# A planned top-k attention with a rational feed-forward layer: 512-wide passes over the first weight matrix, and longer planned TensorE steps for row tiles 8 to 21

## The chip, the cores and the metric

One core of one Trainium2 chip runs the whole kernel as one program. The time is that of the device in microseconds (us), the median of several executions. A profiled execution gives a trace, and its span runs from the first to the last instruction.

## The reference

Attention over 8 batches, 8 heads, 576 positions and a head size of 64, where each row keeps its 32 largest scores, followed by a layer whose activation is a ratio of two polynomials:

```
scores = q @ k.T / 8
kth    = 32nd largest score of each row
attn   = softmax of the scores >= kth
x      = attn @ v                      # heads side by side: 4608 x 512
h      = x @ w_in                      # w_in 512 x 2048, float64
g      = (a0 + a1*h + a2*h^2 + a3*h^3) / (1 + |b0|*|h| + |b1|*h^2 + 1e-6)
out    = g @ w_out                     # w_out 2048 x 512, float64
```

q, k, v, a and b are float32. Both weight matrices arrive as 64-bit words, so the kernel turns them into 32-bit numbers on the chip.

## The kernel before, in words

**Tiles.** A row tile is 128 query rows of one head (a mixed tile: the last 64 rows of two heads). There are 288, numbered in the order of work. TensorE makes a tile's scores (`scores`, lines 577 to 589), ScalarE copies them out of PSUM, and VectorE finds the 32nd largest (lines 595 to 638) and the masked probabilities (line 694). TensorE transposes these (line 792) and multiplies them with v (`multiply`, line 825) for two row blocks of one head pair at a time. Tiles 0 to 15 are the first two row blocks of all eight heads, 16 to 19 are mixed, and 20 begins the next two row blocks.

**The layer.** When all heads of 256 rows are done they form a chunk. A chunk runs in 8 groups: a hidden product with w_in (line 967, three passes with high and low parts), the ratio on ScalarE, GpSimd and VectorE, and a product with w_out (lines 1127 and 1134).

**The weights.** `weight_block` takes one block of 128 x 512 float64 words: 16 blocks of w_in and 16 of w_out. A block of w_in comes in two loads of 128 x 256 words into the tiles that later hold the high and low parts (`win_h`, `win_l`). Then each half takes these steps: `low` (ScalarE, line 393, into a PSUM bank), `high` (VectorE, line 398), `sign` and `size` (ScalarE, lines 404 and 408), `join` (GpSimd, line 412). After both halves the block is split into a high part (line 274 or 276) and a low part (line 434). The PSUM bank is one of the two with the tag "mm", which the transposes, `multiply` and the hidden products also use. It goes back when both `size` steps are done.

**The order.** `Plan` simulates the engines while the program is written. Every step has an engine, a planned length, a key, steps that it waits for, and buffers that it takes and gives. `choose` gives a free engine the ready step with the lowest key. A step that is not critical stands back when a critical one with a lower key comes within LOOK. The order found this way is the fixed order of each engine's queue and of the DMA queue of SyncE (SP); the lengths have no other effect. The key of row tile n is n times T, with T 5.084. The entries of KEY move a kind of step against this: KL the load and split of k, QL that of q and of the mixed tiles' input, VL the load of v, PT the transposes, AV the product with v, EU and EW the ratio, PJ the product with w_out, WL the load of w_out's low parts, MS the later chunks.

**Buffers.** There are two buffers for v (tag "v"), given back by the last product with them (line 894), and one staging buffer for the loads of k and q (tag "kr"), given back when the low part is split off (lines 494 and 534).

Of the kernel before, what the change touches and what calls it, by code (L numbers as in the profile page):

```python
# [17 lines left out]
AX = mybir.AxisListType  # L18
PSUM = bass.MemoryType.PSUM

KEY = {'XM': 1, 'LN': 12, 'UV': 'DVE', 'UK': -552.455, 'B0': ('POOL',), 'B1': ('POOL', 'DVE'), 'B2': ('DVE', 'POOL'), 'B3': ('DVE', 'POOL'), 'WH': ('POOL', 'ACT'), 'XH': ('POOL', 'ACT'), 'TH': 0, 'EU': -5.754, 'HW': 256, 'Q0': ('POOL', 'ACT'), 'Q1': ('POOL',), 'SPLIT': (0, 2, 4, 6), 'XS': 1, 'RH': ('ACT',), 'p2': ('POOL',), 'p4': ('POOL',), 'ratio': ('POOL',), 'ratio_low': ('POOL',), 'URG': -48.538, 'PT': -11.07, 'AV': -5.694, 'MOE': 38.884, 'LOOK': 0.321, 'T': 5.084, 'KL': -2.162, 'PJ': 39.271, 'WL': -16.714, 'EX': 28.932, 'EW': 11.969, 'ALT': {'ACT': 0.086, 'DVE': 78.012, 'POOL': 2.27}, 'WG': 4.183, 'QL': -8.645, 'PACE': 10.97, 'MS': -1.055, 'NM': ('POOL',), 'WD': ('POOL', 'ACT'), 'LP': ('POOL',), 'VL': -3.335}
NEG = -3.0e38
NB = 8

# [154 lines left out]
def tile_topk_attention__then__rational_ffn(  # L179
# [48 lines left out]
    def add(*args, **kwargs):  # L228
        return plan.add(*args, **kwargs)
# [21 lines left out]
    pe_r = lambda n: max(0.109, n / 2230 + 0.003)  # L251
    pe_f = lambda n: 2 * max(0.109, n / 1200 + 0.003)
    pe_t = 0.109
    dma = lambda n, words: max(0.52 * n, words * 4 / 260e3)


# [59 lines left out]
    tiny = const.tile([P, 1], F32, name="tiny")  # L316
    nc.gpsimd.memset(tiny, 1e-9)

    win_h, win_l = {"nm": "win_h"}, {"nm": "win_l"}

    def own(win, c, e):
        def tile_of(dtype=F32R):
            nm = f"{win['nm']}{c}_{e}"
            x = const.tile([P, 512], dtype, tag=nm, name=nm)
            if dtype == F32R:
                win[c, e] = x
            return x
        return tile_of

# [21 lines left out]
    def weight_block(src, r0, e0, split, key, nm):  # L351
        rows = src[r0 : r0 + P, e0 : e0 + 512]
        o = Obj()
        f64 = rows.dtype != F32
        hi, lo, away = split
        plain = lo is None and away is None
        hold = [Hold("t") for _ in range(1 if lo is not None else 2)]
        xhold, turn = Hold("mm", 2), [Hold("wt")]

        def words(i, dtype=F32):  # L360
            return buf(hold[i], [P, 512], dtype, f"w_{nm}_{i}")

        if not f64:

            def load():
                o.w = hi if plain else words(0)
                o.low = words(1, F32R) if away is not None else lo if plain else lo()
                o.hi = hi if plain else hi()
                nc.sync.dma_start(o.w, rows)

            hold = [] if plain else hold
            last = [add("SP", dma(1, P * 512), load, key=key, take=hold)]
        else:

            def load():
                to = [words(i) for i in range(2)] if lo is None else [hi(F32), lo(F32)]
                o.parts = []
                for i, e in enumerate(range(0, 512, 256)):
                    r = to[i].bitcast(I32)
                    nc.sync.dma_start(r, rows[:, e : e + 256].bitcast(I32))  # L380
                    r = r.rearrange("p (e t) -> p e t", t=2)
                    o.parts.append((slice(e, e + 256), r[:, :, 0], r[:, :, 1]))

            ld = add("SP", dma(2, P * 1024), load, key=key, take=hold + turn if lo is None else [])
            last, first, final = [], [], []
            for i in range(2):

                def low(i=i):
                    es, low, high = o.parts[i]
                    if i == 0:  # L390
                        o.bits = bank(xhold, [P, 512], f"wb_{nm}")
                        o.w = words(0) if lo is not None else hi if plain else hi(F32)
                    nc.scalar.activation(o.bits[:, es], low.bitcast(U32), AF.Identity, scale=STEP, bias=two_)

                def high(i=i):
                    es, low, high = o.parts[i]
                    x = o.bits[:, es].bitcast(I32)
                    nc.vector.scalar_tensor_tensor(
                        x, high, 3, x, op0=ALU.logical_shift_left, op1=ALU.bitwise_xor
                    )  # L400

                def sign(i=i):
                    es, low, high = o.parts[i]
                    nc.scalar.activation(high.bitcast(F32), high.bitcast(F32), AF.Sign)

                def size(i=i):
                    es, low, high = o.parts[i]
                    nc.scalar.activation(o.w[:, es], o.bits[:, es], AF.Abs)

                def join(i=i):  # L410
                    es, low, high = o.parts[i]
                    nc.gpsimd.tensor_tensor(
                        out=o.w[:, es], in0=o.w[:, es], in1=high.bitcast(F32), op=ALU.mult
                    )

                s1 = add("ACT", act(256) + 0.15, low, [ld] + first, key + 1,
                         take=[] if first else [xhold] + (hold if lo is not None else []))
                first = [s1]
                s2 = add("DVE", dve(256), high, [s1], key + 1)
                s3 = add("ACT", act_sb(256), sign, [s2], key + 1)  # L420
                s4 = add("ACT", act(256), size, [s2], key + 2, give=[xhold])
                last.append(
                    add("POOL", pool_t(256), join, [s3, s4], key + 2, give=hold[i : i + 1] + turn[0 : i] if plain else [])
                )

        def high_part():
            if lo is not None and f64:
                o.hi, o.low = hi(), lo()
            elif f64:
                o.hi, o.low = words(0, F32R), words(1, F32R)  # L430
            affine(o.hi, o.w, 1.0, 0.0)

        def low_part():
            engine().tensor_tensor(out=o.low, in0=o.w, in1=o.hi.bitcast(F32), op=ALU.subtract)

        def high_again():
            affine(hi(), o.hi.bitcast(F32), 1.0, 0.0)

        if plain:
            return last  # L440

        s = add(one(512, 0, KEY['WH']), None, high_part, last, key + 3)
        if away is None:
            return [add(two(512, *KEY["LP"]), None, low_part, [s], key + 3, give=hold)]
        s = add(two(512, *KEY["LP"]), None, low_part, [s], key + 3)
        steps = [
            add("SP", dma(1, P * 512), lambda: nc.sync.dma_start(away, o.low.bitcast(F32)), [s],
                key + 3, give=hold[1:] + turn if f64 else hold)
        ]
        if f64:  # L450
            steps.append(add(one(512, 0, KEY['WH']), None, high_again, [s], key + 3, give=hold[0:1]))
        return steps
# [3 lines left out]
    def add_weights(key0, gap):  # L456
        n = 0
        blocks = []
        for e in range(0, DFF, 512):
            for c in range(HP):  # L460
                split = *(own(win, c, e // 512) for win in (win_h, win_l)), None
                blocks.append((("i", c, e // 512), w_in, c * P, e, split))
            for f in range(4 * (e // 512), 4 * (e // 512) + 4):
                split = (wout.get(f) or own_out(f), None, wout_l.get(f))
                blocks.append((("o", f), w_out, f * P, 0, split))
        for n, (name, *args) in enumerate(blocks):
            w_steps[name] = weight_block(*args, key0 + n * gap, f"w{n}")
# [97 lines left out]
    def add_tile(t):  # L565
# [131 lines left out]
            )  # L697

        if u.mixed:
            s = add("PE", 2 * pe_f(HF), scores, [kv.mload, prev.s], key - 3.2, take=[shold],  # L700
                    give=[kv.mhold], crit=True)
        else:
            s = add("PE", 0.07 + 4 * pe_r(HF), scores, [kv.load[t.h], u.pair.q.load, prev.s], key - 3.2, take=[shold],
                    give=[kv.khold, u.pair.q.hold], crit=True)
        prev.s = s
        e = add("ACT", act(S), evacuate, [s], key - 2.6, take=[sbhold], give=[shold], crit=True)
# [50 lines left out]
    def add_values(u):  # L757
# [108 lines left out]
        for i in ([0, 2] if u.mixed else [0, 1, 2]):  # L866
# [5 lines left out]
            bh = Hold("mm")  # L872
            n = NJ if i < 2 else 2
            kk = KEY['PT'] + (u.tiles[0].key + T if i == 0 else key + 0.4 * i)
            x = add("PE", n * pe_t, transpose(i), dep, kk, take=[bh] + ([] if at else [thold[i]]))
            tp.append(x)
            x.give = [u.phold]
            if i == 2:
# [10 lines left out]
        m = None  # L889
        cuts = [[0, 1, 2], [3, 4]] if u.mixed or lone else [[0, 1], [2, 3], [4]]  # L890
        for cs in cuts:
            m = add("PE", len(cs) * n_av, multiply(cs), [m] if m else pair.ev + [pair.vload], key + KEY['AV'],
                    take=[] if m else [avh] + ([] if u.chunk.parts or u.mixed else [u.chunk.hold]))
        m.give = [pair.vhold] + [thold[0]] + ([] if u.mixed else [thold[1]])
        m2, n = m, u.nq * len(pair.units)
# [457 lines left out]
```

## Time and profile before

| | |
|---|---|
| Median of 3 runs | 1546.0 us (1544.91 to 1546.16) |
| Profiled execution | 1545.54 us, span 1543.8 us |
| TensorE (PE) busy | 1431.8 us, 93% |
| VectorE (DVE) busy | 1383.6 us, 90% |
| ScalarE (ACT) busy | 1358.1 us, 88% |
| GpSimd (POOL) busy | 1150.2 us, 75% |
| Mean granted TensorE clock | 0.974 |

Engines run beside each other, so a share of busy time says little until it is read stage by stage: in each stage one looks for the engine that is hardly ever idle, and for what the others wait for. PEld is TensorE's weight load, which overlaps its matmuls. "A <- B" in a list of waits says that the engine sat idle before A until B was done. "idle before" stands in brackets behind a row of a timeline. A clock of 1.00 is the full 2.4 GHz and 0.50 is 1.2 GHz.

### The profile page before, as it was taken

Reading aid. Unit: us, or ns where it says so; the run is one execution under the profiler, and the core shown is the slowest. Engines: PE = TensorE matmul, PEld = TensorE weight load, DVE = VectorE, ACT = ScalarE, POOL = GpSimd, SP = SyncE. Lnnn points to the kernel's source line nnn. Section 1 sums busy time; section 2 is a strip of 40 time slices with the busy share of each in tenths; the row PEclk is TensorE's granted clock in tenths of the full one; section 3 lists DMA queues with packets and bytes.
Section 4 is the critical chain, followed back from the end, with each engine's and each line's share of the span. In section 5 each row is a group of like instructions: output and inputs, shape, how many; then the busy total and the mean of one; then the engine's idle time right before and its main releaser. Section 6 shows DMA issues by size and latency. Waiting matters only on the chain.

```text
span 1543.8 us, 31629 instructions
## 1 busy us (share of the span) xinstructions
PE 1431.8 (93%) x9537; PEld 1126.8 (73%) x9537; DVE 1383.6 (90%) x5492; ACT 1358.1 (88%) x2600; POOL 1150.2 (75%) x1668
## 2 busy tenths in 40 slices
PE   1557799999999999999999999999999999999996
PEld 1335577877777778788778788787787777877874
DVE  6888899999999999999999999999999999996342
ACT  6878898989998999999899989999998989887763
POOL 6777788768877787778877887778788988876120
PEclk9767999999999999999999999999999999999998
DMA  7643234222422244223422342224322342211211
GB/s 233 202 130 115 73 120 142 70 69 75 140 87 74 82 121 130 66 69 104 131 78 63 93 138 82 68 87 128 108 63 76 100 148 67 73 49 50 57 51 49
DMA packets 91796, 148.95 MB, mean 96 GB/s; under 512 B 13536, under 2 KB 39136, under 8 KB 91616
## 3 DMA queue, kind: packets, MB, share of 16 engines
q1 hardware_dynamic: 91552, 146.84, 31.8%
q8 instruction: 78, 1.28, 0.4%
q14 instruction: 102, 0.84, 0.2%
q0 software_dynamic: 64, 0.00, 0.0%
HBM read 134.22 MB, written 12.58 MB: 95 GB/s over the span
## 4 chain that ended last, share of the span: by engine, by line
PE 80%; DVE 6%; ACT 6%; POOL 4%; DMA 2%; issue 1%; SPq 0%; POOLq 0%; ACTq 0%
PE ph_m L967 21%; PE po_m L1127 12%; PE av L825 11%; PE po_m L1134 10%; PE s L586 8%; PE trp L792 8%; PE ph_t L967 3%; PE s L583 2%; PE po_t L1127 2%; PE po_t L1134 1%; DVE m L629 1%; DVE pr L612 1%; DVE pr L694 1%; PE trp L795 1%; DVE x L637 1%
## 5 line engine op out<-in xcount | busy, mean ns | idle before, releaser
L967 PE MATMUL ph_m<-xh_m,win_h 128*128 128x256 f32 x1024 | 316.7, 309 | 3.3 <-ACT p L811 1.8
L629 DVE MAX8 m<-x 128x8 f32<-128x192 f32 (+1 forms) x864 | 309.5, 358 | 2.1
L967 PE MATMUL ph_m<-xh_m,win_l 128*128 128x256 f32 x1024 | 287.2, 280 | 0.0
L967 PE MATMUL ph_m<-xl_m,win_h 128*128 128x256 f32 x1024 | 286.9, 280 | 0.0
L792 PE MATMUL trp<-ident,pr 128*128 128x128 f32 x1312 | 225.1, 281 | 37.4 <-ACT p L811 12.1
L586 PE MATMUL s<-k,q 128*128 128x288 f32 x1024 | 208.1, 327 | 52.2 <-POOL k L494 36.9
L811 ACT COPY p<-trp 128x512 f32<-128x512 f32 (+1 forms) x448 | 228.9, 513 | 28.9 <-PE trp L792 18.9
L1127 PE MATMUL po_m<-wout,pa_m 128*128 128x512 f32 x512 | 250.1, 595 | 0.0
L792 PEld LDWEIGHTS trp<-ident,pr 128*128 128x128 f32 x1312 | 163.7, 144 | 102.4 <-issue 26.1
L694 DVE SCALAR_TENSOR_TENSOR pr<-sb,m,e 128x576 f32<-128x576 f32 x288 | 230.4, 800 | 4.8 <-ACT e L691 3.3
L691 ACT ACTIVATE e<-sb,st 128x576 f32<-128x576 f32 x288 | 218.3, 758 | 13.1 <-POOL st L282 5.9
L593 ACT COPY sb<-s 128x576 f32<-128x576 f32 x288 | 186.1, 646 | 45.8 <-PE s L586 33.1
L612 DVE TENSOR_TENSOR pr<-s,sb 128x192 f32<-128x192 f32 x576 | 198.7, 347 | 26.2 <-ACT sb L593 22.5
L586 PEld LDWEIGHTS s<-k,q 128*128 128x128 f32 x1024 | 155.5, 197 | 84.8 <-POOL k L494 38.6
L967 PEld LDWEIGHTS ph_m<-xh_m,win_h 128*128 128x128 f32 x1024 | 193.8, 189 | 21.3 <-issue 6.7
L967 PEld LDWEIGHTS ph_m<-xl_m,win_h 128*128 128x128 f32 x1024 | 194.1, 190 | 8.2 <-issue 6.3
L618 DVE MAX8 x<-pr 128x8 f32<-128x192 f32 x576 | 199.5, 346 | 0.0
L637 DVE MATCH_REPLACE8 x<-m,x 128x192 f32<-128x192 f32 x576 | 198.7, 345 | 0.0
L967 PEld LDWEIGHTS ph_m<-xh_m,win_l 128*128 128x128 f32 x1024 | 193.1, 189 | 0.0
L825 PE MATMUL av<-p,vm 128*64 128x256 f32 (+1 forms) x1920 | 184.6, 341 | 1.5 <-ACT p L811 1.1
L825 PEld LDWEIGHTS av<-p,vm 128*64 128x64 f32 x1920 | 110.8, 141 | 75.4 <-issue 9.4
L1021 POOL TENSOR_TENSOR pa_m<-pa_m,va_m 128x512 f32<-128x512 f32 x88 | 113.3, 1287 | 39.5 <-ACT va_m L1018 37.4
(152 smaller groups left out, 3632.3 us busy)
## 6 DMA issues: line engine op xcount, KB each, us to landing
wl_m<-wout_l SPq DMA_DIRECT2D x128, 256.0 KB, 2.7
vm<-in_v_dram SPq DMA_DIRECT2D x96, 320.0 KB, 2.9
kx<-in_qk_dram SPq DMA_DIRECT2D x64, 288.0 KB, 2.9
qx<-in_qk_dram SPq DMA_DIRECT2D x64, 256.0 KB, 2.8
km<-in_qk_dram SPq DMA_DIRECT2D x32, 352.0 KB, 3.3
w_w<-in_moe_w_out_dram SPq DMA_DIRECT2D x32, 256.0 KB, 4.0
out_dram<-ob_m SPq DMA_DIRECT2D x64, 128.0 KB, 1.7
win_h<-in_moe_w_in_dram SPq DMA_DIRECT2D x16, 256.0 KB, 5.6
```

The lines of the kernel that those rows point to most:

```text
L586: nc.tensor.matmul(s[:, hf, 0:HF], u.pair.q.q[:, i, t.h, o : o + P], kv.k[:, t.h, cols], start=(i == 0), stop=(i == 1),)
L612: engine().tensor_tensor(out=to, in0=one_, in1=two_, op=op)
L618: nc.vector.max(t.x[:, o : o + 8], t.w[:, 2 * i * TH :][:, 0:TH])
L629: nc.vector.max(t.m[:, 8 * r : 8 * r + 8], src)
L637: nc.vector.match_replace(y, t.m[:, 8 * r : 8 * r + 8], x, NEG)
L691: nc.scalar.activation(t.e, t.sb, AF.Exp, scale=SCALE, bias=t.st)
L694: nc.vector.scalar_tensor_tensor(out=t.pr, in0=t.sb, scalar=t.kth, in1=t.e, op0=ALU.is_ge, op1=ALU.mult, accum_out=u.ss[:, t.h : t.h + 1],)
L792: nc.tensor.transpose(u.ps[i][:, c * P : (c + 1) * P], u.pr[:, x], ident)
L811: nc.scalar.copy(pair.pT[i][:, at].rearrange("p c n -> p (c n)")[:, 0:nw], u.ps[i][:, 0:nw])
L825: nc.tensor.matmul(pair.av[d, 0 : u.nq * len(pair.units)], lhs, x[:, 0, d] if u.mixed else x[:, 0] if lone else x, start=(c == 0), stop=(c ...
L967: nc.tensor.matmul(y.ph[:, f * NT : (f + 1) * NT], w[c, ff][:, at : at + P], z[:, c, :], start=(c == 0 and i == 0), stop=(c == HP - 1 and ...
L1127: nc.tensor.matmul(o.po[i], y.pa[:, at], wout[ff], start=(ff == 0), stop=(ff == NF - 1),)
```

## The change

There are three edits. A block of w_in is loaded by one DMA into one tile of 128 x 2 x 512 words, which later holds both parts, and every pass over it is 512 wide instead of two of 256. The blocks of w_out keep two halves. In the plan, the scores, transposes and products with v of tiles 8 to 21 get 1.8 times their length. Thirteen numbers in KEY change. B0, which also changes, is used only by a second plan, which runs when a flag asks for it.

```diff
-KEY: 'B0': ('POOL',), 'EU': -5.754, 'PT': -11.07, 'AV': -5.694, 'LOOK': 0.321, 'KL': -2.162, 'PJ': 39.271,
-     'WL': -16.714, 'EW': 11.969, 'ALT': {'ACT': 0.086, ...}, 'QL': -8.645, 'MS': -1.055, 'VL': -3.335
+KEY: 'B0': ('ACT',), 'EU': -8.21, 'PT': -8.847, 'AV': -14.568, 'LOOK': 0.282, 'KL': -1.482, 'PJ': 34.415,
+     'WL': -15.67, 'EW': 11.854, 'ALT': {'ACT': 0.085, ...}, 'QL': -6.982, 'MS': -1.501, 'VL': -16.625
...
+    cold = lambda n: 1.8 if not full and 8 <= n < 22 else 1.0
...
-    win_h, win_l = {"nm": "win_h"}, {"nm": "win_l"}
-    def own(win, c, e):
+    win_h, win_l = {}, {}
+    def own_in(c, e):
         def tile_of(dtype=F32R):
-            nm = f"{win['nm']}{c}_{e}"
-            x = const.tile([P, 512], dtype, tag=nm, name=nm)
+            nm = f"win{c}_{e}"
+            x = const.tile([P, 2, 512], dtype, tag=nm, name=nm)
             if dtype == F32R:
-                win[c, e] = x
+                win_h[c, e], win_l[c, e] = x[:, 0], x[:, 1]
             return x
...
             def load():
-                to = [words(i) for i in range(2)] if lo is None else [hi(F32), lo(F32)]
                 o.parts = []
+                if lo is not None:
+                    r = lo(F32).rearrange("p t n -> p (t n)").bitcast(I32)
+                    nc.sync.dma_start(r, rows.bitcast(I32))
+                    r = r.rearrange("p (e t) -> p e t", t=2)
+                    o.parts.append((slice(0, 512), r[:, :, 0], r[:, :, 1]))
+                    return
...
+            np, nw = (1, 512) if lo is not None else (2, 256)
+            xhold.users = np
-            for i in range(2):
+            for i in range(np):
...
-                s1 = add("ACT", act(256) + 0.15, low, [ld] + first, key + 1,
+                s1 = add("ACT", act(nw) + 0.0006 * nw, low, [ld] + first, key + 1,
...
-            s = add("PE", 2 * pe_f(HF), scores, ...
+            s = add("PE", cold(t.n) * 2 * pe_f(HF), scores, ...
-            s = add("PE", 0.07 + 4 * pe_r(HF), scores, ...
+            s = add("PE", cold(t.n) * (0.07 + 4 * pe_r(HF)), scores, ...
-            x = add("PE", n * pe_t, transpose(i), ...
+            x = add("PE", cold(u.tiles[0].n) * n * pe_t, transpose(i), ...
-            m = add("PE", len(cs) * n_av, multiply(cs), ...
+            m = add("PE", cold(u.tiles[0].n) * len(cs) * n_av, multiply(cs), ...
```

## Rows read from the trace of the kernel before

**Rows 1.** The page, busy time: engine, us, share of the span, instructions.
```profile
PE 1431.8 (93%) x9537; PEld 1126.8 (73%) x9537; DVE 1383.6 (90%) x5492; ACT 1358.1 (88%) x2600; POOL 1150.2 (75%) x1668
```

**Rows 2.** Busy us by stage: stage, length, PE, PEld, DVE, ACT, POOL, clock, DMA, GB/s.
```profile
16.00:60.00 44.00, 18.78 (x76) 13.35 (x76) 37.94 (x145) 36.18 (x86) 35.47 (x52) 1.00 0.72 230
60.00:140.00 80.00, 46.71 (x202) 30.65 (x203) 68.21 (x261) 62.35 (x148) 59.52 (x95) 0.63 0.42 132
140.00:200.00 60.00, 46.27 (x316) 37.85 (x315) 52.58 (x211) 53.38 (x115) 46.72 (x71) 0.90 0.34 99
200.00:300.00 100.00, 95.61 (x687) 75.19 (x688) 94.65 (x383) 93.77 (x183) 80.68 (x121) 1.00 0.35 111
300.00:1400.00 1100.00, 1093.83 (x7529) 869.16 (x7529) 1071.84 (x4396) 1018.37 (x1911) 886.65 (x1282) 1.00 0.31 91
1400.00:1531.00 131.00, 130.62 (x733) 100.60 (x731) 54.09 (x88) 87.46 (x148) 33.34 (x32) 1.00 0.18 53
...
300.00:600.00 300.00, 294.85 (x2035) 231.81 (x2035) 292.78 (x1210) 276.63 (x520) 236.38 (x348) 1.00 0.33 96
```

**Rows 3.** TensorE's waits, 0 to 200 us: us in total, times, longest.
```profile
PE s L586 <- POOL k L494: 36.9, 6, 16.1
PE s L586 <- DVE x L612: 12.7, 7, 4.3
PE trp L792 <- ACT w_w L408: 11.1, 5, 2.9
```

**Rows 4.** TensorE in order of time: start, length in us, what, idle before.
```profile
94.08 1.33 PE L586 MATMUL s<-k,q 128*128 128x288 f32 x4 [0.21 <-POOL k L494]
...
96.57 4.47 PE L825 MATMUL av<-p,vm 128*64 128x256 f32 x20 [0.53 <-ACT p L811]
100.97 0.80 PE L586 MATMUL s<-k,q 128*128 128x288 f32 x4
...
106.47 1.30 PE L586 MATMUL s<-k,q 128*128 128x288 f32 x4 [4.26 <-DVE x L612]
...
201.19 2.38 PE L825 MATMUL av<-p,vm 128*64 128x256 f32 x20
```

**Rows 5.** Groups by line and form, 0 to 200 us: count, busy us, mean ns.
```profile
L393 ACT ACTIVATE wb_w<-win_h,two 128x256 f32<-128x256 uint32 x16 | 7.9, 495 | 8.0 <-DMA win_h<-in_moe_w_in_dram 7.9
L404 ACT ACTIVATE win_h<-win_h 128x256 f32<-128x256 f32 x16 | 7.0, 440 | 1.7 <-DVE wb_w L398 1.7
L408 ACT ACTIVATE w_w<-wb_w 128x256 f32<-128x256 f32 x32 | 11.6, 375 | 0.1
L811 ACT COPY p<-trp 128x512 f32<-128x512 f32 x28 | 16.4, 587 | 7.1 <-PE trp L792 6.9
L811 ACT COPY p<-trp 128x256 f32<-128x256 f32 x11 | 4.1, 375 | 0.8 <-PE trp L800 0.8
L398 DVE SCALAR_TENSOR_TENSOR wb_w<-win_h,wb_w 128x256 int32<-128x256 int32 x16 | 6.8, 423 | 15.6 <-ACT wb_w L393 15.6
L412 POOL TENSOR_TENSOR w_w<-w_w,win_h 128x256 f32<-128x256 f32 x16 | 11.8, 736 | 10.6 <-ACT w_w L408 10.5
L434 POOL TENSOR_TENSOR win_l<-w_w,win_h 128x512 fp32r<-128x512 f32 x16 | 20.4, 1274 | 1.8 <-ACT win_h L274 1.4
```

**Rows 6.** The chain of waits, 0 to 200 us: shares of the stretch by line.
```profile
by line: PE av L825 7.4%; PE s L586 6.7%; issue 6.7%; PE trp L792 6.7%; DMA win_l<-in_moe_w_in_dram 6.3%; ACT wb_w L393 5.6%; DVE pr L612 3.6%; PE s L583 3.2%; ACT p L811 3.2%; DVE wb_w L398 3.2%; ACT e L691 3.1%; PE ph_m L967 3.1%; DVE m L
```

**Rows 7.** The start, all engines in order of time.
```profile
10.57 0.49 ACT L393 ACTIVATE wb_w<-win_l,two 128x256 f32<-128x256 uint32 x1 [0.17 <-DMA win_l<-in_moe_w_in_dram]
...
13.16 0.73 POOL L412 TENSOR_TENSOR w_w<-w_w,win_l 128x256 f32<-128x256 f32 x1
13.87 0.67 POOL L276 TENSOR_SCALAR k<-kx 128x576 fp32r<-128x576 f32 x1
...
16.08 1.33 PE L586 MATMUL s<-k,q 128*128 128x288 f32 x4 [16.08 <-POOL k L494]
```

**Rows 8.** Waits of SP's DMA queue, 0 to 200 us: total, times, longest.
```profile
SPq L549 <- PE av L825: 38.9, 9, 8.2
```

More of the change, by code (lines that the diff above doesn't have):

```diff
@@ L19 @@
 PSUM = bass.MemoryType.PSUM
-KEY = {'XM': 1, 'LN': 12, 'UV': 'DVE', 'UK': -552.455, 'B0': ('POOL',), 'B1': ('POOL', 'DVE'), 'B2': ('DVE', 'POOL'), 'B3': ('DVE', 'POOL'), 'WH': ('POOL', 'ACT'), 'XH': ('POOL', 'ACT'), 'TH': 0, 'EU': -5.754, 'HW': 256, 'Q0': ('POOL', 'ACT'), 'Q1': ('POOL',), 'SPLIT': (0, 2, 4, 6), 'XS': 1, 'RH': ('ACT',), 'p2': ('POOL',), 'p4': ('POOL',), 'ratio': ('POOL',), 'ratio_low': ('POOL',), 'URG': -48.538, 'PT': -11.07, 'AV': -5.694, 'MOE': 38.884, 'LOOK': 0.321, 'T': 5.084, 'KL': -2.162, 'PJ': 39.271, 'WL': -16.714, 'EX': 28.932, 'EW': 11.969, 'ALT': {'ACT': 0.086, 'DVE': 78.012, 'POOL': 2.27}, 'WG': 4.183, 'QL': -8.645, 'PACE': 10.97, 'MS': -1.055, 'NM': ('POOL',), 'WD': ('POOL', 'ACT'), 'LP': ('POOL',), 'VL': -3.335}
+KEY = {'XM': 1, 'LN': 12, 'UV': 'DVE', 'UK': -552.455, 'B0': ('ACT',), 'B1': ('POOL', 'DVE'), 'B2': ('DVE', 'POOL'), 'B3': ('DVE', 'POOL'), 'WH': ('POOL', 'ACT'), 'XH': ('POOL', 'ACT'), 'TH': 0, 'EU': -8.21, 'HW': 256, 'Q0': ('POOL', 'ACT'), 'Q1': ('POOL',), 'SPLIT': (0, 2, 4, 6), 'XS': 1, 'RH': ('ACT',), 'p2': ('POOL',), 'p4': ('POOL',), 'ratio': ('POOL',), 'ratio_low': ('POOL',), 'URG': -48.538, 'PT': -8.847, 'AV': -14.568, 'MOE': 38.884, 'LOOK': 0.282, 'T': 5.084, 'KL': -1.482, 'PJ': 34.415, 'WL': -15.67, 'EX': 28.932, 'EW': 11.854, 'ALT': {'ACT': 0.085, 'DVE': 78.012, 'POOL': 2.27}, 'WG': 4.183, 'QL': -6.982, 'PACE': 10.97, 'MS': -1.501, 'NM': ('POOL',), 'WD': ('POOL', 'ACT'), 'LP': ('POOL',), 'VL': -16.625}
 NEG = -3.0e38
@@ L366, in load @@
                 o.w = hi if plain else words(0)
-                o.low = words(1, F32R) if away is not None else lo if plain else lo()
-                o.hi = hi if plain else hi()
+                o.low = words(1, F32R) if away is not None else lo
+                o.hi = hi if plain else hi() if lo is None else lo()[:, 0]
                 nc.sync.dma_start(o.w, rows)
@@ L375, in load @@
             def load():
-                to = [words(i) for i in range(2)] if lo is None else [hi(F32), lo(F32)]
                 o.parts = []
+                if lo is not None:
[4 more added lines that the diff above has]
+                    return
                 for i, e in enumerate(range(0, 512, 256)):
-                    r = to[i].bitcast(I32)
+                    r = words(i).bitcast(I32)
                     nc.sync.dma_start(r, rows[:, e : e + 256].bitcast(I32))
@@ L382, in load @@
                     o.parts.append((slice(e, e + 256), r[:, :, 0], r[:, :, 1]))
-            ld = add("SP", dma(2, P * 1024), load, key=key, take=hold + turn if lo is None else [])
+            np, nw = (1, 512) if lo is not None else (2, 256)
+            xhold.users = np
+            ld = add("SP", dma(np, P * 1024), load, key=key, take=hold + turn if lo is None else [])
             last, first, final = [], [], []
-            for i in range(2):
+            for i in range(np):
                 def low(i=i):
@@ L414, in join @@
                     )
-                s1 = add("ACT", act(256) + 0.15, low, [ld] + first, key + 1,
+                s1 = add("ACT", act(nw) + 0.0006 * nw, low, [ld] + first, key + 1,
                          take=[] if first else [xhold] + (hold if lo is not None else []))
                 first = [s1]
-                s2 = add("DVE", dve(256), high, [s1], key + 1)
-                s3 = add("ACT", act_sb(256), sign, [s2], key + 1)
-                s4 = add("ACT", act(256), size, [s2], key + 2, give=[xhold])
+                s2 = add("DVE", dve(nw), high, [s1], key + 1)
+                s3 = add("ACT", act_sb(nw), sign, [s2], key + 1)
+                s4 = add("ACT", act(nw), size, [s2], key + 2, give=[xhold])
                 last.append(
-                    add("POOL", pool_t(256), join, [s3, s4], key + 2, give=hold[i : i + 1] + turn[0 : i] if plain else [])
+                    add("POOL", pool_t(nw), join, [s3, s4], key + 2, give=hold[i : i + 1] + turn[0 : i] if plain else [])
                 )
         def high_part():
-            if lo is not None and f64:
-                o.hi, o.low = hi(), lo()
+            if lo is not None:
+                x = lo()
+                o.hi, o.low = x[:, 0], x[:, 1]
             elif f64:
@@ L460, in add_weights @@
             for c in range(HP):
-                split = *(own(win, c, e // 512) for win in (win_h, win_l)), None
+                split = None, own_in(c, e // 512), None
                 blocks.append((("i", c, e // 512), w_in, c * P, e, split))
@@ L699, in add_tile @@
         if u.mixed:
-            s = add("PE", 2 * pe_f(HF), scores, [kv.mload, prev.s], key - 3.2, take=[shold],
+            s = add("PE", cold(t.n) * 2 * pe_f(HF), scores, [kv.mload, prev.s], key - 3.2, take=[shold],
                     give=[kv.mhold], crit=True)
         else:
-            s = add("PE", 0.07 + 4 * pe_r(HF), scores, [kv.load[t.h], u.pair.q.load, prev.s], key - 3.2, take=[shold],
+            s = add("PE", cold(t.n) * (0.07 + 4 * pe_r(HF)), scores, [kv.load[t.h], u.pair.q.load, prev.s], key - 3.2, take=[shold],
                     give=[kv.khold, u.pair.q.hold], crit=True)
@@ L874, in add_values @@
             kk = KEY['PT'] + (u.tiles[0].key + T if i == 0 else key + 0.4 * i)
-            x = add("PE", n * pe_t, transpose(i), dep, kk, take=[bh] + ([] if at else [thold[i]]))
+            x = add("PE", cold(u.tiles[0].n) * n * pe_t, transpose(i), dep, kk, take=[bh] + ([] if at else [thold[i]]))
             tp.append(x)
@@ L891, in add_values @@
         for cs in cuts:
-            m = add("PE", len(cs) * n_av, multiply(cs), [m] if m else pair.ev + [pair.vload], key + KEY['AV'],
+            m = add("PE", cold(u.tiles[0].n) * len(cs) * n_av, multiply(cs), [m] if m else pair.ev + [pair.vload], key + KEY['AV'],
                     take=[] if m else [avh] + ([] if u.chunk.parts or u.mixed else [u.chunk.hold]))
```

## The prediction

> **What bounds the kernel now.** I read the page's busy times first. TensorE is busy for 93% of the span, VectorE for 90% and ScalarE for 88% [rows 1], so the shares alone do not say which engine sets the end. The stages do [rows 2]. From 300 to 1400 us TensorE is idle for 1100 - 1093.83 = 6.2 us, from 200 to 300 us for 4.4 us, and from 1400 to 1531 us for 0.4 us, although VectorE has little left to do by then. So from 200 us on TensorE is the bound, and the end comes when it has done its work. It loses time before that: 25.2 us of idling from 16 to 60 us, 33.3 us from 60 to 140 us and 13.7 us from 140 to 200 us. Its clock also falls to a mean of 0.63 between 60 and 140 us. A gain there moves the end by as much, as long as TensorE stays full afterwards; a gain on another engine after 200 us moves nothing.
>
> The list of TensorE's waits up to 200 us shows what it lacked [rows 3]: 36.9 us for the low part of k, of which 16.1 us is the very start; 12.7 us for scores that VectorE had not yet read; and 11.1 us in which a transpose waited for `size` of a w_in block, because that block held one of the two "mm" banks. The chain of waits in the same stretch [rows 6] has no owner: `low` of the weight blocks has 5.6% of it, `high` 3.2%.
>
> The change touches this stretch in three ways. I add them up on the profiled execution, 1545.54 us with a span of 1543.8 us; the median of the runs is 0.46 us higher, and I add that at the end.
>
> **1. The 512-wide passes.** Per w_in block, ScalarE now spends 2 x (495 + 440 + 375) = 2620 ns on `low`, `sign` and `size` [rows 5]. A pass of 512 columns is not in the trace for these. From below, a copy on the same engine grows from 375 to 587 ns when it goes from 256 to 512 columns, so 256 more columns cost 212 ns; from above, a double pass costs twice the single one. I take the first, since it is the same engine and the same widths: 707 + 652 + 587 = 1946 ns. That saves 674 ns a block, 10.8 us over 16 blocks, between 0 and 10.8 us. GpSimd's `join` goes from 2 x 736 to about 1274 ns, a row of the same operation at 512: 3.2 us less. VectorE's `high` has no row at two widths: between nothing and one of two passes, 16 x 423 ns = 6.8 us; I take nothing. 16 of the loads also leave SP's queue; since no wait in the rows ends there, I count that at nothing.
>
> Little of this lies on the path. The chain spends 5.6% of 200 us = 11.2 us on `low`, half of it for w_in, as the two matrices have as many passes. One pass for two takes 283 of 990 ns off, 29%: 1.6 us (bounds 0 and 10.8). The bank is held from the first `low` to the last `size`; ScalarE's share of that shrinks by 674/2620 = 26%, so of the 11.1 us of waiting I take off 2.9 us (bounds 0 and 11.1). What is late next there is the evacuation of the transposes, on the same ScalarE.
>
> Against it stands the start. The first k is split by GpSimd behind the first block's `join`, which ended at 13.89 us, and TensorE's first scores wait for that [rows 7]. One pass begins only when the whole block is there, at 10.57 us, and runs in series: 0.71 + 0.85 + 0.65 + 0.59 + 1.27 = 4.07 us, to 14.64 us. That is 0.7 us later. If the steps overlap as the halves do, it is nothing. I take +0.7 us.
>
> The Trainium skill speaks against this edit: "Perfetto Trace Analysis", section "Optimizing Scalar/DVE Operations", holds that grouping helps a saturated engine, while on one that is not saturated but causes bubbles elsewhere, smaller instructions may let work finish sooner. ScalarE is busy for 62.35 of 80 us from 60 to 140 us and does cause such bubbles [rows 2, 3]. By that rule alone only the +0.7 us would stand of this part, and the sum below would be -1.1 us; by the rows, the bank comes free only after the last half, so the earlier end of the first half buys nothing.
>
> **2. Lengths of TensorE in the plan.** Lengths only set the order. A wide product with v is planned with 5 x 4.1 x 0.109 = 2.23 us; it took 2.38 us at 201 us, but 4.47 us at 96.57 us [rows 4]. With 1.8 the plan has 4.02 us, so its error falls from 2.24 to 0.45 us, 1.79 us a product. Two wide products fall under the edit (heads 4 to 7 of the first rows): 3.6 us. The place where that error hurts is SP's queue, in which a load of v waits for a product to free its buffer, 38.9 us in nine waits [rows 8], and the loads of k queue behind it; k's low part then comes late for the scores. Apart from the start those waits are 36.9 - 16.1 = 20.8 us, the upper bound; from below, a pessimistic plan can also put useful steps too late, by as much as the error that it removes, 3.6 us. I take half of 3.6 us as gain, 1.8 us, because the plan can use the knowledge only where another load is ready to go first.
>
> The clock itself does not follow tile numbers. Four scores of tile 13 took 1.33 us, those of tile 14, right behind 20 products, 0.80 us, and those of tile 15, after an idle gap of 4.26 us, 1.30 us [rows 4]: both levels, 1.2 and 2.4 GHz, lie inside the range of the edit.
>
> **3. The moved keys.** Products with v become more urgent by 8.9 (1.7 tiles of 5.084), loads of v by 13.3 (2.6 tiles), the ratio's first steps by 2.5, the product with w_out by 4.9; transposes become less urgent by 2.2, loads of q by 1.7 and of k by 0.7. After 200 us these can win at most the idle time left there, 4.4 + 6.2 + 0.4 = 11.0 us. For a loss I take the worst steady stretch, 300 to 600 us, with 5.15 us idle in 300 [rows 2]: at that rate 1331 us hold 22.8 us, 11.9 us more than now. No row favours either side, and while TensorE is full its order does not matter; I take 0. Cover for that is the queue of layer groups: if it runs empty, the loss is the 11.9 us.
>
> **Sum.** -1.6 - 2.9 + 0.7 - 1.8 = -5.6 us: 1539.9 us for the profiled execution, 1540.4 us on the scale of the median. I say 1540.
>
> **Rivals.**
> *A. No change, 1546 us.* What ScalarE and the plan win early is given back before TensorE is full: from 60 to 140 us VectorE is busy for 68.2 of 80 us [rows 2], and each tile must pass it. If VectorE sets the pace until 200 us, earlier banks only lengthen the waits for scores, the 12.7 us of rows 3. Against: VectorE was idle for 11.8 us in that stretch too.
>
> *B. Loads of v block those of k, 1553 us.* With its key 2.6 tiles earlier, a load of v stands ahead of loads of k and q in SP's queue and waits there until a product frees one of the two buffers. A wait was 38.9/9 = 4.3 us on average, 8.2 at most [rows 8]. It decides from two such loads in front of a needed k (8.6 us against the 5.6 us won); three cost 13.0 us: 1545.5 - 5.6 + 13.0 + 0.5 = 1553.4 us. For: the waits are already there with the later key. Against: the plan places such a load only when its own clock says that the buffer is free, and the product itself is now more urgent.
>
> *C. A warm TensorE, 1529 us.* If the new order feeds TensorE evenly enough to keep 2.4 GHz from 60 to 140 us, the 46.71 us of busy time there shrink by 37%, 17.3 us: 1545.5 - 17.3 + 0.5 = 1528.7 us. For: the clock rose right behind each wide product [rows 4]. Against: 33.3 us of idling lie in the stretch, and the sum removes only a sixth of them. The Trainium skill has this as a rule ("TensorE: Matmul & The Clock Gate", section "Loop structure matters more than you think"): whether matmuls run warm is settled by how the loops feed them. By that rule the fixed 1.8 would be too pessimistic as soon as the feeding gets better; the rows above agree that both levels occur within the range.
>
> **How the numbers follow.** Forecast 0.42, A 0.18, B 0.24, C 0.16. This kernel's measurement tells about 0.2%, 3.1 us, from no change. Forecast and C are faster: 0.58; A is the same: 0.18; B is slower: 0.24. The forecast's own range is 1534 to 1543 us: below, twice the gains of part 1 and the whole 3.6 us of part 2 (-9.0 + 0.7 - 3.6 = -11.9 us); above, the end of what counts as faster. The whole range reaches to C and to B, 1527 to 1554 us; the loss of 11.9 us after 200 us, 1552 us with the forecast's gain, lies inside.
>
> **What would show it.** The profile after should show 16 `low` passes of w_in at about 0.71 us and 16 `join` at 1.27 us; under 9 us of transposes waiting for w_in's `size`; first scores between 16 and 17 us; less than 20 us of waits for k's low part after the start; and TensorE's idle time before 200 us some 6 us below 88 us, with 11 us after 200 us as before. A is right if that idle time is unchanged. B is right if SP's waits of v's loads for the product grow beyond 38.9 us and scores wait longer for k. C is right if the clock from 60 to 140 us rises well above 0.63. The forecast is wrong, whatever the total, if the time moved after 200 us.

## The result: 1532 us, and where the 12 us of the profile lie

The changed kernel takes 1532.1 us (median of 5 runs, 1529.8 to 1535.4); the kernel before took 1546.1 us beside it. The ratio is 0.990, with a 95% interval of 0.9886 to 0.9914. I had said 1540, with a range of 1527 to 1554: faster, as forecast, but by 14.0 us where the sum gave 5.6.

The page's busy times of the changed kernel answer to [rows 1]; its span is 1531.4 us, 12.4 us less.

```profile
PE 1428.4 (93%) x9537; PEld 1123.7 (73%) x9537; DVE 1375.5 (90%) x5476; ACT 1353.2 (88%) x2557; POOL 1145.2 (75%) x1648
```

The stages of the changed kernel answer to [rows 2] (stage, length, then busy us of PE, PEld, DVE, ACT and POOL, clock, DMA share, GB/s):

```profile
16.00:60.00 44.00, 18.30 (x76) 12.80 (x76) 35.35 (x128) 37.58 (x76) 40.85 (x51) 1.00 0.72 232
60.00:140.00 80.00, 47.99 (x230) 32.16 (x230) 74.06 (x281) 66.58 (x142) 66.21 (x101) 0.66 0.47 148
140.00:200.00 60.00, 50.36 (x352) 41.02 (x351) 56.52 (x233) 53.95 (x112) 44.63 (x69) 0.89 0.30 90
200.00:300.00 100.00, 98.33 (x696) 77.61 (x695) 96.57 (x394) 92.03 (x176) 80.83 (x120) 1.00 0.36 104
300.00:1400.00 1100.00, 1095.45 (x7544) 869.28 (x7543) 1063.62 (x4376) 1019.10 (x1916) 881.63 (x1273) 1.00 0.32 91
```

The two tables can be subtracted. Up to 200 us TensorE idles for 83.3 us in place of 88.2. From 200 to 1400 us it idles for 6.2 us in place of 10.6. Its busy time falls by 3.4 us with the same 9537 matmuls, so they ran a little faster; the end is unchanged. 4.9 + 4.4 + 3.4 - 0.2 (the end) are about the 12.4 us. Up to 200 us TensorE has now issued 656 matmuls, where it had issued 593.

TensorE's waits up to 200 us answer to [rows 3]:

```profile
PE s L595 <- POOL k L503: 26.4, 4, 18.1
PE trp L801 <- ACT wout L416: 17.9, 8, 4.4
PE trp L801 <- ACT p L820: 8.8, 11, 2.0
PE s L595 <- DVE x L621: 7.4, 4, 3.0
...
PE s L592 <- ACT w_w L416: 3.9, 1, 3.9
...
PE trp L801 <- ACT w_w L416: 1.6, 2, 1.2
```

Two more lines of the list of the kernel before are needed beside it:

```profile
PE trp L792 <- ACT p L811: 9.5, 13, 1.3
PE trp L792 <- ACT wout L408: 6.4, 3, 4.6
```

Outside the start, the waits for k fell from 20.8 to 8.3 us. The waits of transposes for w_in's `size` (`w_w`) fell from 11.1 to 1.6 us, but those for w_out's `size` (`wout`), 6.4 us before, became 17.9 us: together they went from 17.5 to 19.5 us, and scores now wait 3.9 us for w_in's `size` as well.

The passes over w_in answer to [rows 5] (busy us, mean ns):

```profile
L401 ACT ACTIVATE wb_w<-win,two 128x512 f32<-128x512 uint32 x16 | 11.7, 732 | 8.7 <-DMA win<-in_moe_w_in_dram 8.4
L412 ACT ACTIVATE win<-win 128x512 f32<-128x512 f32 x16 | 10.8, 677 | 2.9 <-DVE wb_w L406 2.8
L416 ACT ACTIVATE w_w<-wb_w 128x512 f32<-128x512 f32 x16 | 9.6, 599 | 0.0
L406 DVE SCALAR_TENSOR_TENSOR wb_w<-win,wb_w 128x512 int32<-128x512 int32 x16 | 11.0, 686 | 13.2 <-ACT wb_w L401 13.0
L420 POOL TENSOR_TENSOR w_w<-w_w,win 128x512 f32<-128x512 f32 x16 | 20.6, 1292 | 5.7 <-ACT w_w L416 5.7
```

And the start in order of time, which answers to [rows 7]:

```profile
13.24 1.28 POOL L420 TENSOR_TENSOR w_w<-w_w,win 128x512 f32<-128x512 f32 x1 [4.28 <-ACT w_w L416]
14.61 0.62 POOL L277 TENSOR_SCALAR win<-w_w 128x512 fp32r<-128x512 f32 x1
15.31 1.28 POOL L443 TENSOR_TENSOR win<-w_w,win 128x512 fp32r<-128x512 f32 x1
16.67 1.41 POOL L503 TENSOR_TENSOR k<-kx,k 64x576 fp32r<-64x576 f32 x1
...
18.13 1.33 PE L595 MATMUL s<-k,q 128*128 128x288 f32 x4 [18.13 <-POOL k L503]
```

### The profile page after: what moved, and what is told of

It reads as the page before. It is cut to its first block, busy times and chain, and to the rows that moved or that the text cites. A ratio compares the mean times of both kernels' runs of the same rounds, so it can differ in the third digit from the quotient of the medians.

```text
span 1531.4 us, 31524 instructions
## 1 busy us (share of the span) xinstructions
PE 1428.4 (93%) x9537; PEld 1123.7 (73%) x9537; DVE 1375.5 (90%) x5476; ACT 1353.2 (88%) x2557; POOL 1145.2 (75%) x1648
## 4 chain that ended last, share of the span: by engine, by line
PE 79%; ACT 9%; DVE 5%; POOL 3%; DMA 3%; issue 2%; SPq 0%; POOLq 0%; ACTq 0%; DVEq 0%
PE ph_m L976 20%; PE po_m L1136 13%; PE po_m L1143 11%; PE av L834 10%; PE trp L801 8%; PE s L595 8%; PE ph_t L976 3%; PE s L592 2%; PE po_t L1136 2%; PE po_t L1143 1%; DMA out_dram<-ob_m 1%; ACT e L700 1%; ACT sb L602 1%; ACT p L820 1%; DVE m L638 1%
## 5 line engine op out<-in xcount | busy, mean ns | idle before, releaser
L976 PE MATMUL ph_m<-xh_m,win 128*128 128x256 f32 x2048 | 443.5, 294 | 2.7 <-ACT p L820 1.9
L976 PEld LDWEIGHTS ph_m<-xh_m,win 128*128 128x128 f32 x2048 | 336.4, 188 | 23.1 <-ACT p L820 8.9
L976 PE MATMUL ph_m<-xl_m,win 128*128 128x256 f32 x1024 | 286.1, 279 | 0.0
L801 PE MATMUL trp<-ident,pr 128*128 128x128 f32 x1312 | 224.9, 281 | 35.7 <-ACT wout L416 17.9
L976 PEld LDWEIGHTS ph_m<-xl_m,win 128*128 128x128 f32 x1024 | 193.4, 189 | 8.3 <-issue 6.2
L998 POOL TENSOR_TENSOR pa_m<-pa_m,hh_m 128x512 f32<-128x512 f32 x88 | 113.4, 1289 | 39.9 <-ACT pa_m L995 37.8
L1004 POOL TENSOR_TENSOR pa_m<-pa_m,h_m 128x512 f32<-128x512 f32 x88 | 113.4, 1289 | 15.8 <-ACT h_m L1001 13.3
```

The lines of the kernel that those rows point to most:

```text
L801: nc.tensor.transpose(u.ps[i][:, c * P : (c + 1) * P], u.pr[:, x], ident)
L976: nc.tensor.matmul(y.ph[:, f * NT : (f + 1) * NT], w[c, ff][:, at : at + P], z[:, c, :], start=(c == 0 and i == 0), stop=(c == HP - 1 and ...
```

## The experiments

Each kernel was timed in five rounds beside the kernel before, whose median on those chips was 1547.4 to 1548.3 us; ratios are to it. All diffs are against the changed kernel unless it says otherwise.

### The parts by themselves

**e1: passes alone.** Old KEY, and `cold` gives 1.0.
```diff
-    cold = lambda n: 1.8 if not full and 8 <= n < 22 else 1.0
+    cold = lambda n: 1.0 if not full and 8 <= n < 22 else 1.0
-KEY: (new numbers)
+KEY: (old numbers)
```


> The kernel before with the 512-wide passes over w_in alone. Theory 1 (each part works by itself; the passes take 10 us off ScalarE and shorten the time that a bank is held): about 1542 us, transposes wait under 6 us for w_in's size instead of 11.1 us. Theory 2 (the parts work mainly by giving another order, and any new order moves the time by several us either way): a time that has nothing to do with the 10 us, anywhere from 1530 to 1560 us, and the bank waits only move to other steps. Theory 3 (the keys carry the gain): 1546 us within 3 us.


Measured: 1562.0 us, ratio 1.0091 (1.0077 to 1.0105). Slower by 14 us. Theories 1 and 3 are wrong here, and the time lies just beyond the wide range of theory 2. Transposes wait 6.6 us for w_in's `size`, where theory 1 had under 6.

**e2: lengths alone.** The kernel before with `cold` in its four places.


> The kernel before with the 1.8 for tiles 8 to 21 alone. Theory 1: about 1544 us, with less than the 20.8 us of waits for k's low part after the start. Theory 2: from 1530 to 1560 us, with a sign that can't be told beforehand. Theory 3: 1546 us within 3 us.


Measured: 1548.6 us, ratio 0.9999 (0.9989 to 1.0009). No change: theory 1 is wrong, theories 2 and 3 both allow it.

**e3: keys alone.** The kernel before with the new KEY.


> The kernel before with the changed numbers of KEY alone. Theory 1: 1546 us within 3 us, idle time of TensorE after 200 us near 11 us. Theory 2: from 1530 to 1560 us; numbers fitted to another order may well be worse here, above 1549 us. Theory 3: 1532 to 1540 us, with idle time after 200 us under 8 us.


Measured: 1558.8 us, ratio 1.0068 (1.0054 to 1.0082). Slower by 10 us: theories 1 and 3 are wrong, theory 2 named the sign.

**e4: without the keys.** The old KEY.


> The changed kernel with the old numbers of KEY, so passes and lengths together. Theory 1: 1532 to 1537 us, near the sum of the two single runs. Theory 2: not the sum of the two single runs, off by more than 4 us. Theory 3: 1543 us or more.


Measured: 1546.8 us, ratio 0.9993 (0.9984 to 1.0003). The two single runs would give 1562 to 1563 us; so the parts do not add, and theory 1 is wrong.

**e5: without the lengths.** `cold` gives 1.0.


> The changed kernel with the factor 1.8 set to 1.0, so passes and keys together. So far passes alone took 14 us more than before, keys alone 10 us more, lengths alone nothing, passes and lengths together nothing. Theory 4 (passes and keys pay only where the plan has true lengths for the slow stretch, since otherwise loads of v wait longer for their product in SP's queue): 1555 us or more, and over 42 us of those waits up to 200 us. Theory 2 (any new order moves the time by several us, with no rule): anywhere from 1530 to 1565 us. Theory 1 (parts add up): 1532 - 0 = 1532 us.


Measured: 1543.2 us, ratio 0.9975 (0.9963 to 0.9987). Two parts that lose 14 and 10 us alone win 4 us together, without the lengths. Theory 4 is wrong as well: its waits are 38.4 us, where it had over 42. So is theory 1.

**e6: without the passes.** The kernel before with lengths and new KEY.


> The kernel before with the lengths and the keys, without the 512-wide passes. Theory 4: 1540 to 1548 us, better than the keys alone by over 10 us, as with the passes; under 40 us of waits of v's loads for their product. Theory 2: anywhere from 1530 to 1565 us. Theory 1 (parts add up): keys alone plus lengths alone, 1557 to 1560 us.


Measured: 1552.8 us, ratio 1.0035 (1.0023 to 1.0048). It is 0.3% faster than the keys alone, where theory 4 had over 10 us and theory 1 no gain; both are wrong. Theory 2 allows it, but its range of 35 us allows almost any time; the nudges below test it more closely.

### A change without purpose

**e7 and e8: a nudge.**
```diff
-'MOE': 38.884
+'MOE': 39.5
```


> The kernel before with one number of the plan nudged, MOE from 38.884 to 39.5, which changes the order of a few steps and has no purpose. Theory 2: off by more than 4 us, with other waits before 200 us. Theories 1 and 4: 1546 us within 3 us, since no step is longer and no load later by rule.


Measured on the kernel before: 1554.4 us, ratio 1.0049 (1.0036 to 1.0062).

> The changed kernel with the same nudge, MOE from 38.884 to 39.5. Theory 2: slower than 1532 us by more than 4 us, since the changed kernel's order is one lucky draw. Theories 1 and 4: 1532 us within 3 us.


Measured on the changed kernel: 1540.8 us, ratio 0.9961 (0.9947 to 0.9974), against 0.990 without the nudge. A number changed for no reason cost 0.5% in one kernel and 0.6% in the other. Theories 1 and 4 had no change and are wrong. The size that theory 2 named is met, but not its place, as the stages of the two nudged kernels show, the one of before first:

```profile
200.00:300.00 100.00, 96.66 (x694) 76.24 (x693) 95.46 (x384) 94.57 (x185) 81.30 (x122) 1.00 0.36 108
300.00:1400.00 1100.00, 1087.75 (x7475) 864.55 (x7475) 1071.59 (x4400) 1009.06 (x1892) 879.57 (x1278) 1.00 0.31 91
```

```profile
200.00:300.00 100.00, 98.41 (x695) 77.25 (x695) 96.09 (x388) 93.94 (x176) 81.43 (x121) 1.00 0.35 102
300.00:1400.00 1100.00, 1091.14 (x7505) 866.26 (x7504) 1068.44 (x4385) 1018.12 (x1914) 875.58 (x1266) 1.00 0.32 91
```

TensorE's idle time up to 200 us stayed (88.2 to 88.0 us, and 83.3 to 81.3 us); that from 200 to 1400 us rose from 10.6 to 15.6 us and from 6.2 to 10.4 us.

### The same order, other durations or banks

**e9: halves in order.** Each of the five steps over w_in emits two instructions of 256 columns, as shown for `size`; the order on every queue stays.
```diff
+            pieces = lambda es: [slice(k, k + 256) for k in range(0, es.stop - es.start, 256)]
-                    nc.scalar.activation(o.w[:, es], o.bits[:, es], AF.Abs)
+                    for k in pieces(es):
+                        nc.scalar.activation(o.w[:, es][:, k], o.bits[:, es][:, k], AF.Abs)
...
```


> The changed kernel with its order kept on every queue: each 512-wide step over w_in is issued as two instructions of 256 columns, one behind the other. So only the durations go back: about 10 us of ScalarE's time, 2.6 us of VectorE's and 3 us of GpSimd's over the 16 blocks. Theory 1 (the passes gain by being shorter): 1536 to 1542 us. Theory 2 (what the passes gained is the order that came with them): 1532 us within 3 us.


Measured: 1537.1 us, ratio 0.992 (0.9905 to 0.9934), against 0.990 (0.9886 to 0.9914). The time lies in theory 1's range, but the kernel before took 2 us more beside it as well, and by the ratios neither theory is ruled out. The shorter durations are worth some 3 us (0.2%), if anything: the intervals overlap, so not even the sign is shown. In the profiles, TensorE's idle time is the same in both, 83.5 against 83.3 us up to 200 us and 6.0 against 6.2 us from there to 1400 us; the difference lies in its busy time, 1432.4 against 1428.4 us. From 60 to 140 us its mean granted clock was 0.60 here and 0.66 in the changed kernel. That the shorter durations shorten TensorE's waiting in total is not seen.

**e10: other banks for the first 20 weight blocks.**
```diff
-                        o.bits = bank(xhold, [P, 512], f"wb_{nm}")
+                        tag = "o" if int(nm[1:]) < 20 else "mm"
+                        o.bits = ps.tile([P, 512], F32, tag=f"{tag}_{xhold.slot}", name=f"wb_{nm}")
```


> The changed kernel with its order kept on every queue: the first 20 weight blocks put their bits into the two banks that the products with w_out use later, instead of the two that the transposes use. Theory 1 (waits for a bank are on the path): the 17.9 us in which transposes wait for size of the w_out blocks, and most other waits for a bank of the weights, go, and the time falls to between 1520 and 1527 us. Theory 2 (a wait removed in a fixed order gives way to the next one): TensorE then waits for k, for VectorE or for the evacuation of the transposes instead, 1529 us or more.


Measured: 1532.2 us, ratio 0.9886 (0.9871 to 0.9902): not told apart from the changed kernel. TensorE's waits up to 200 us in this kernel:

```profile
PE s L596 <- POOL k L504: 29.9, 4, 18.4
PE trp L802 <- ACT p L821: 9.8, 12, 1.9
PE trp L802 <- DVE pr L704: 8.6, 5, 4.6
PE s L596 <- DVE x L622: 7.6, 4, 3.0
...
PE trp L802 <- ACT wout L417: 2.9, 3, 1.3
```

The 17.9 us for w_out's `size` fell to 2.9 us, and TensorE's idle time before 200 us is 82.6 us, where it was 83.3: the waits for k grew by 3.5 us, those for the probabilities by 4.9 us, and several others by 1.0 to 2.3 us each. A wait was removed and the next one stood behind it, as theory 2 had it.

**e11: the same edit on the kernel before.**


> The kernel before with the same edit and its own order kept: the 17.5 us in which transposes wait for size of the weight blocks should go. Theory 1: 1534 to 1541 us. Theory 2: 1544 us or more.


Measured: 1545.5 us, ratio 0.9982 (0.9973 to 0.9991): 2.8 us faster, out of 17.5 us of waits that it takes aim at. Of these 3.5 us are left, and the waits for the evacuated transposes grew from 9.5 to 16.3 us:

```profile
PE s L587 <- POOL k L495: 38.1, 7, 15.9
PE trp L793 <- ACT p L812: 16.3, 13, 3.6
...
PE trp L793 <- ACT w_w L409: 3.5, 2, 2.4
```

TensorE's idle time before 200 us is the same 88.2 us. Theory 2 holds here too.

### The keys where TensorE is full

**e12: new keys from the second batch on.**
```diff
+        KEY.update(EARLY)           # the old numbers
         for n, u in enumerate(units):
+            if u.bi == 1:
+                KEY.update(LATER)   # the new numbers of EU, PT, AV, KL, PJ, WL, EW, QL, MS, VL
```


> The changed kernel with the old numbers of KEY for the first batch's steps and the new ones for all later batches (LOOK and ALT stay old); TensorE's queue is that of the run without the keys for its first 890 rows. That run had 79.6 us of TensorE idle before 200 us and 17.6 us from 200 to 1400 us. Theory 5 (lengths save idle time before 200 us, and the keys that suit the rest save it after 200 us, each by itself): idle time before 200 us stays near 80 us, that from 200 to 1400 us falls to 6 to 9 us, and the time is 1530 to 1537 us. Theory 2 (the order after 200 us is a draw that no key set wins by itself): 10 to 20 us idle after 200 us, 1538 us or more.


Measured: 1547.3 us, ratio 0.9997 (0.9985 to 1.0009); 82.1 us of idle time before 200 us and 15.8 us from 200 to 1400 us. Theory 5 is right about the first and wrong about the second: the new keys do not save time after 200 us by themselves. Whether LOOK or ALT, which stayed old, would, was not tried.

### All of them by stage

Every span is TensorE's busy time and its idle time. From the stages of each profile, in us:

| run | span | busy | idle to 200 | idle 200 to 1400 | idle from 1400 |
|---|---|---|---|---|---|
| before | 1543.8 | 1431.8 | 88.2 | 10.6 | 13.2 |
| e1 passes | 1562.6 | 1437.2 | 89.1 | 20.3 | 16.0 |
| e2 lengths | 1547.2 | 1437.5 | 83.2 | 13.1 | 13.4 |
| e3 keys | 1557.0 | 1438.4 | 90.4 | 14.4 | 13.8 |
| e4 passes, lengths | 1548.3 | 1436.1 | 79.6 | 17.6 | 15.0 |
| e5 passes, keys | 1544.1 | 1430.5 | 91.4 | 8.1 | 14.1 |
| e6 lengths, keys | 1550.2 | 1436.0 | 86.1 | 14.6 | 13.5 |
| all three | 1531.4 | 1428.4 | 83.3 | 6.2 | 13.4 |
| e7 before, nudged | 1550.1 | 1433.5 | 88.0 | 15.6 | 13.0 |
| e8 all, nudged | 1539.6 | 1432.6 | 81.3 | 10.4 | 15.2 |
| e9 halves in order | 1535.3 | 1432.4 | 83.5 | 6.0 | 13.4 |
| e10 other banks | 1530.9 | 1427.2 | 82.6 | 6.9 | 14.2 |
| e11 before, other banks | 1543.6 | 1431.2 | 88.2 | 10.8 | 13.4 |
| e12 keys later | 1544.8 | 1431.2 | 82.1 | 15.8 | 15.6 |

The column up to 200 us has a rule in it. With the lengths it is lower in all four pairs: by 5.0 us (before and e2), 9.5 (e1 and e4), 4.3 (e3 and e6) and 8.1 (e5 and all three). The nudges move it by 0.2 and 2.0 us. The new keys raise it in all four pairs, but only by 2.2 to 3.7 us. The column from 200 to 1400 us follows no single part: it goes from 6.0 to 20.3 us, and a nudge moves it by 4 to 5 us. Among the eight combinations the two lowest are those with passes and new keys together, 8.1 and 6.2 us, against 10.6 to 20.3 us; but e8 and e12, which have both too (e12 from the second batch on), stand at 10.4 and 15.8 us, so that the pair is the reason is not shown. Where the order is the same, it is within 0.7 us of the kernel whose order it is (e9 and e10; e11).

Each row is one execution, and the clock varies between executions of one kernel: beside e9 to e11 the kernel before ran from 1546.3 us at a mean granted clock of 0.975 to 1552.7 us at 0.969. So a few us in the busy column need no cause in the order. In part the column goes with the clock in the profile itself. e1 has 1437.2 us for the same matmuls; from 200 to 300 us it idles for 9.2 us, and its granted clock in that stage is 0.97 where before and after have 1.00:

```profile
200.00:300.00 100.00, 90.79 (x623) 70.06 (x623) 85.30 (x338) 88.17 (x173) 76.44 (x110) 0.97 0.35 100
```

## Why the prediction was right, and where it was not

**What bounds the kernel: right, with a limit.** From 200 to 1400 us TensorE was idle for 1% of the time or less in both kernels. But what is won early does not always come out at the end: e2 and e4 have 5.0 and 8.6 us less idle time before 200 us and are not faster than the kernel before, since more idle time after 200 us and more busy time took the gain back.

**The size: partly luck.** The sum put 5.6 us before 200 us, and 4.9 us of idle time were won there. But the passes, which had most of the 5.6 us, show nothing in that column when the order is held (e9), and the lengths, which had 1.8 us, show 4.3 to 9.5 us. The other 4.4 us of idle and 3.4 us of busy time come from places where the sum had nothing.

**Durations of the passes: right.** 732, 677 and 599 ns stand against 707, 652 and 587, 1292 against 1274, so ScalarE saves 2620 - 2008 = 612 ns a block, 9.8 us. VectorE's `high`, which I counted at no gain, saves 160 ns a block (686 against 2 x 423), 2.6 us.

**Their worth on the path: wrong.** I had 1.6 us from the chain and 2.9 us from the banks. e9 finds some 3 us for all shorter durations at once, with intervals that overlap and with none of it in TensorE's idle time. The step "of the 11.1 us of waiting I take off 2.9 us" failed: the waits moved to w_out's blocks. In a fixed order, taking away 14.0 of 17.5 us of such waits was worth 2.8 us (e11), and taking away 15.0 of 17.9 us nothing that can be told from the changed kernel (e10). I had treated one name in a list of waits as a price; it was the last of several things that were late together.

**The rule on smaller instructions.** The Trainium skill ("Perfetto Trace Analysis", section "Optimizing Scalar/DVE Operations") holds that breaking up instructions may help where an engine that is not saturated causes bubbles elsewhere. In one order, broken instructions did not help (ratio 0.992 against 0.990), so no run here bears the rule out. In e9 each half stands right behind the other, and halves with other steps between them were not tried in the same order.

**The start: the sign right, the cause wrong.** First scores came 2.05 us later, not 0.7. `join` ended at 14.52 us, as the serial sum said (14.64). But GpSimd then took the high and low parts of the block ahead of k's low part, which I had not looked for. That goes with the keys and not with the passes: the block's low part stands ahead of k's in every run that has the new keys from the start, the keys alone (e3, first scores at 18.36 us) among them, and behind it in every run with the old keys, e4 with its 512-wide passes (16.44 us) among them. KL, which makes the split of k less urgent, is one of the moved numbers; it was not tried by itself. The block's low part and k's, first in e3, then in e4:

```profile
15.56 1.27 POOL L434 TENSOR_TENSOR win_l<-w_w,win_h 128x512 fp32r<-128x512 f32 x1
16.91 1.40 POOL L494 TENSOR_TENSOR k<-kx,k 64x576 fp32r<-64x576 f32 x1
```

```profile
14.98 1.40 POOL L503 TENSOR_TENSOR k<-kx,k 64x576 fp32r<-64x576 f32 x1
16.46 1.29 POOL L443 TENSOR_TENSOR win<-w_w,win 128x512 fp32r<-128x512 f32 x1
```

**The lengths: the place right, the gain mis-sized, the path not shown.** I had 1.8 us; idle time before 200 us falls by 4.3 to 9.5 us in four pairs. The total is lower with the lengths in three of the pairs (ratio 0.9993 against 1.0091, 1.0035 against 1.0068, 0.990 against 0.9975) and the same in the fourth (e2). Waits of v's loads for their product fall in the same pairs, by 5.8, 6.4, 15.1 and 2.3 us; here is the wait in SP's queue up to 200 us of the changed kernel, which answers to [rows 8]:

```profile
SPq L558 <- PE av L834: 36.1, 9, 5.9
```

The last of the four differences, 2.3 us, is no more than the order-keeping e9 moves this wait (38.4 us). And the second link that I had named, k's low part coming earlier, did not follow: the waits for it after the start fall by 2.6, 0.8 and 1.1 us in three pairs and rise from 1.3 to 8.3 us in the fourth. So the queue is one place where the longer planned lengths help, but how that turns into less idle time stays open.

**The keys and the order: wrong.** "While TensorE is full its order does not matter; I take 0" is the step that failed. By my own test, the forecast is wrong where time moves after 200 us, and 4.4 of the 9.3 us of idle time won up to 1400 us lie there. The bound of 11.9 us was the useful part: e1's 9.7 us more idle time from 200 to 1400 us lies inside it. And the sum had no term for how the three edits work on one another, which is the largest thing found: +14, 0 and +10 us alone, -14 us together.

**The rivals.** A is wrong, since idle time before 200 us fell. B is wrong for the whole change, with waits of 36.1 us, not over 38.9; but the passes alone and the keys alone have 46.9 and 48.3 us of them and are the two slowest runs, which is a hint and no more, as the third slowest, e7, has 38.2 us. C is wrong: the clock from 60 to 140 us rose only from 0.63 to 0.66.

What stays open is why this order leaves only 6.2 us of idle time from 200 to 1400 us. The runs show that it does, that a nudge takes it to 10.4 us, and that none of the three edits brings it alone. One rival was not tested: the new numbers may have been picked because their order happened to be fast, and then most small moves would lose. One nudge in one direction cannot tell.

## What to carry to other kernels

Where a planner fixes the order, an edit has two effects, on the durations and on the order, and only a run with the order held still tells them apart; here the durations were worth some 3 of the 14 us, if anything. Before a step of a few tenths of a per cent is put down to its purpose, nudge a number without purpose: here that alone moved the time by 0.5%. A planned length that is nearer the truth in a slow stretch is worth having: it is the one part that lowered idle time there in every combination, though the total only in three of four.

## What the runs showed of the hardware

The clock of 1.00 in the first stage is not a granted clock that was recorded. From 16 to 60 us it is 1.00 in both kernels [rows 2], yet four scores at 18.13 us of the changed kernel took 1.33 us, as they did at 94.08 us of the kernel before, where the mean clock was 0.50 from 90 to 100 us; at 100.97 us, behind the wide product, they took 0.80 us [rows 4]. The clock entries in the two traces begin only at 53.1 us (before) and 53.6 us (changed), each during a wide product with v; ahead of that there is no entry, and the profile counts the time as 1.00. By their durations the first scores ran at the 1.2 GHz level. In the changed kernel that holds for the scores of tiles 0 to 5 (1.30 to 1.33 us each), which the longer planned lengths leave out; a range that takes them in was not tried.
